# Fourier sums and folds in parts of 128 tokens behind each transposed block, and masked scores with their row minimum from one VectorE operation per head pair

## The chip, the cores and the metric

One core of one Trainium2 chip runs the whole program. The metric is the time of one execution on the device, in microseconds (us); the kernel before was timed in three runs.

## What is computed

Three layers follow each other: attention over a window of 64 tokens (4 batches, 8 heads, 576 tokens, 64 columns per head), a Fourier layer with a multilayer perceptron, and a gated perceptron. Cut to what matters here:

```python
scores = np.where((rel >= 0) & (rel < 64), 0.125 * (q @ k.T), -1e9)
attn = np.exp(scores - scores.max(-1, keepdims=True))
attn = attn / (attn.sum(-1, keepdims=True) + 1e-9)
x = (attn @ v), heads side by side                # [4, 576, 512]
u = x + real(fft(fft(x, axis=1), axis=2))         # tokens, then columns
un = (u - mean(u)) / sqrt(var(u) + 1e-6)
y = u + max(un @ w_ch1, 0) @ w_ch2
```

and a second perceptron with a gate over the tokens follows on `y`.

## The kernel before

The first stage, about a fifth of the time, runs attention as the main lane (`attention`, L303) and two other lanes that fill it: the decoding of the first weights, and the Fourier layer and normalization (`dft`, L439, and `ln`, L577) of the batches that are done. `drive` (L1060) interleaves the lanes by costs that the generators yield, and a list scheduler then sets the final order on each engine. Each engine's queue is worked in that order.

Attention goes through 36 blocks `n` of 64 queries, nine per batch. `scores(n)` (L308) lets TensorE (PE) compute four head pairs of 128 x 128 scores into one tile `sc`; VectorE (DVE) scales and masks all four at once (L317, 128 x 512) and takes the row maximum, negated, of all four at once (L320); ScalarE (ACT) then runs four exponentials with that maximum as bias (L322). `transposes` (L325) turns the four results on PE into `pt`, and ACT copies them (L331). `pv` (L334) multiplies two blocks with the values, `norm` (L346) divides on DVE, and `xt` (L365) transposes 128 finished tokens (64 for the last part of a batch, so five parts per batch) into the one PSUM tile `xt`, from which ACT copies them into `uT` (L373). `uT` holds all tokens with the 512 columns on four slices of 128 partitions.

`dft(b)` begins when all of batch b stands in `uT`. DVE makes the sums `E` and differences `O` of the two column halves over all 576 tokens (L448, L449: 128 x 1152), then folds the token axis in place (L452, L464: 128 x 576). ACT and GpSimd (POOL) split each result into two float32r parts, `eh`/`el` and `oh`/`ol` (L457, L458, L465, L466). One row more, `grow`, comes from `O` over POOL, ACT and POOL (L461 to L463). Then PE does the first Fourier stage: for each of three token groups a sum of seven matrix products (L482 with `grow` first, then six over `mm3`, L124 to L126) and then one of six with `oh`. The copies of these sums, `cp`, are written over `E` and `O` (L490). The second stage (L496) ends in `mi` and `pl`, which are added into `uT` (L512 to L521).

After the attention stage come the two perceptrons, which fill the rest with matrix products.

Of the kernel before, what the change touches and what calls it, by code (L numbers as in the profile page):

```python
# [13 lines left out]
ALU = mybir.AluOpType  # L14
# [93 lines left out]
class Kernel:  # L108
# [194 lines left out]
    def attention(self):  # L303
# [4 lines left out]
        def scores(n):  # L308
            b, j = divmod(n, NB)
            q, k = self.qt.pop((b, j)), self.kt[b, j // 3]  # L310
            sc = ps.tile([128, 4, 128], F32, tag="sc", bufs=2, name="sc")
            for hp in range(4):
                o = 64 * (j % 3)
                nc.tensor.matmul(sc[:, hp], lhsT=q[:, hp].rearrange("p a b -> p (a b)"), rhs=k[:, hp, o:o + 128], start=True, stop=True)  # L314
            mx = p.tile([128, 4], F32, tag="mx", bufs=3, name="mx")
            s = p.tile([128, 4, 128], F32, tag="s", bufs=SB, name="s")
            nc.vector.scalar_tensor_tensor(  # L317
                out=s, in0=sc, scalar=0.125, in1=self.mask[:, int(j == 0)].unsqueeze(1).to_broadcast([128, 4, 128]),
                op0=ALU.mult, op1=ALU.add)
            nc.vector.tensor_reduce(out=mx, in_=s, axis=AX.X, op=ALU.max, negate=True)  # L320
            for hp in range(4):
                nc.scalar.activation(out=s[:, hp], in_=s[:, hp], func=AF.Exp, bias=mx[:, hp:hp + 1])  # L322
            st[n], st['mx'] = s, mx
# [41 lines left out]
        def xt(n):  # L365
# [6 lines left out]
            t0 = S * b + 128 * i  # L372
            nc.scalar.activation(out=self.uT[:, :, t0:t0 + m], in_=t[:, :, 0:m], func=AF.Copy)  # L373
            if j == NB - 1:
                self.xdone = b
# [35 lines left out]
    def open_dft(self):  # L411
        nc = self.nc
        self.dp, self.dft_es = self.pool("dft", side="left")
        p = self.dp
        self.xdone = -1
        w = [516, 516, 512, 512, 258, 870, 870, 870, 870]
# [15 lines left out]
    def load_tables(self, i, after):  # L432
# [4 lines left out]
        self.tc.keep_in_program_order(self.nc.gpsimd.dma_start(self.tab[:, c], self.aps["tab"][:, c]))  # L437

    def dft(self, b):  # L439
        nc, p = self.nc, self.dp  # L440
        x = self.uT[:, :, S * b:S * b + S]
        V, G, A = nc.vector, nc.gpsimd, nc.scalar
        EF = G if b in FP else V
        row = p.tile([1, S], F32, tag="row", name="row")
        nc.sync.dma_start(row, x[0:1, 2])
        E = p.tile([128, 2, S], F32, tag="E", name="E")
        O = p.tile([128, 2, S], F32, tag="O", name="O")
        EF.tensor_tensor(out=E, in0=x[:, 0:2], in1=x[:, 2:4], op=ALU.add)  # L448
        EF.tensor_tensor(out=O, in0=x[:, 0:2], in1=x[:, 2:4], op=ALU.subtract)  # L449
        fold = lambda t: t[:, :, 1:289]  # L450
        rev = lambda t: t[:, :, 575:287:-1]
        EF.tensor_tensor(out=fold(E), in0=fold(E), in1=rev(E), op=ALU.add)  # L452
        eh = p.tile([128, 2, 290], F32R, tag="eh", name="eh")
        el = p.tile([128, 2, 290], F32R, tag="el", name="el")
        oh = p.tile([128, 2, 290], F32R, tag="oh", name="oh")
        ol = p.tile([128, 2, 290], F32R, tag="ol", name="ol")
        A.activation(out=eh[:, :, 0:289], in_=E[:, :, 0:289], func=AF.Copy)  # L457
        G.tensor_tensor(out=el[:, :, 0:289], in0=E[:, :, 0:289], in1=eh[:, :, 0:289], op=ALU.subtract)  # L458
        gr = p.tile([1, 290], F32, tag="gr", name="gr")
        G.tensor_copy(gr[:, 0:1], O[0:1, 0, 0:1])  # L460
        G.tensor_tensor(out=gr[:, 1:289], in0=O[0:1, 0, 1:289], in1=O[0:1, 0, 575:287:-1], op=ALU.add)  # L461
        A.activation(out=self.grow[0:1, 0:289], in_=gr[:, 0:289], func=AF.Copy)
        G.tensor_tensor(out=self.grow[32:33, 0:289], in0=gr[:, 0:289], in1=self.grow[0:1, 0:289], op=ALU.subtract)  # L463
        EF.tensor_tensor(out=fold(O), in0=fold(O), in1=rev(O), op=ALU.subtract)  # L464
        A.activation(out=oh[:, :, 0:289], in_=O[:, :, 0:289], func=AF.Copy)  # L465
        G.tensor_tensor(out=ol[:, :, 0:289], in0=O[:, :, 0:289], in1=oh[:, :, 0:289], op=ALU.subtract)  # L466
        yield 5000
# [6 lines left out]
        for which in range(2):  # L474
            for i, (t0, t1) in enumerate(ts):
# [3 lines left out]
                if which:  # L479
                    self.mm3(ps[:m, 0:n], [(oh[:, c, t0:t1], ol[:, c, t0:t1], self.sdh[:, c], self.sdl[:, c]) for c in range(2)])  # L480
                else:
                    nc.tensor.matmul(ps[:m, 0:n], lhsT=self.grow[:, t0:t1], rhs=self.gt, start=True, stop=False)  # L482
                    self.mm3(ps[:m, 0:n], [(eh[:, c, t0:t1], el[:, c, t0:t1], self.cdh[:, c], self.cdl[:, c]) for c in range(2)], first=False)
                if i < 2:
                    hi, lo = (bh, bl) if which else (ah, al)
                    hi, lo = hi[:, i, 0:n], lo[:, i, 0:n]
                else:
                    t = bt if which else at
                    hi, lo = t[0:33, 0:n], t[64:97, 0:n]
                cp = (O if which else E)[:m, i // 2, 288 * (i % 2):288 * (i % 2) + n]  # L490
                A.activation(out=cp, in_=ps[:m, 0:n], func=AF.Copy)
                A.activation(out=hi, in_=cp, func=AF.Copy)
                G.tensor_tensor(out=lo, in0=cp, in1=hi, op=ALU.subtract)
                yield 1700

        def stage2(out, lo_, hi_, tail, ch, cl, sl):  # L496
# [846 lines left out]
```

## Time and profile before

| | |
|---|---|
| median of 3 runs | 779.79 us (777.94 to 780.92) |
| the profiled execution | 780.66 us, of which 778.9 us are the span from the first to the last instruction |
| PE busy | 755.9 us, 97% of the span |
| DVE busy | 491.1 us, 63% |
| ACT busy | 340.5 us, 44% |
| POOL busy | 219.2 us, 28% |
| mean granted TensorE clock | 0.991 |

An engine's busy time is the time in which it had an instruction under way; matrix products overlap each other in the record, so a busy PE is not PE at its peak. [...] A wait names the instruction whose end released the waiting one.

### The profile page before, as it was taken

How to read it: one execution, taken by the hardware profiler on the slowest of the kernel's cores; microseconds unless marked ns; L12 is line 12 of the kernel's file. 1: busy time of each engine (PE TensorE's matmuls, PEld its weight loads, DVE VectorE, ACT ScalarE, POOL GpSimd, SP SyncE). 2: the span in 40 equal slices, each digit the busy share in tenths (PEclk: the TensorE clock that was granted, in tenths of full speed). 3: DMA queues.
4: the chain of work that ended last, by engine and by line, in shares of the span. 5: the costliest groups of instructions: out<-in, count | busy, mean ns of one | idle time of the engine just before them, and what ended most of it. 6: DMA issues, size and time to landing. Idle time of an engine off the chain costs nothing.

```text
span 778.9 us, 13646 instructions
## 1 busy us (share of the span) xinstructions
PE 755.9 (97%) x5018; PEld 727.3 (93%) x5018; DVE 491.1 (63%) x1126; ACT 340.5 (44%) x807; POOL 219.2 (28%) x268
## 2 busy tenths in 40 slices
PE   8879899999999999999999999999999999999998
PEld 7779688889999999999999999999999898989898
DVE  5677959594346489794588767644700468574662
ACT  5678797764233666341235323322742343130310
POOL 2135535534203551053712111121591021010100
PEclk9989999999999999999999999999999999999999
DMA  9996672353005878567746943953410020204023
GB/s 275 341 257 182 202 213 69 107 164 122 1 1 157 290 237 322 194 243 262 256 180 232 341 171 104 363 230 109 133 56 1 0 70 12 72 21 142 7 75 121
DMA packets 84770, 123.35 MB, mean 158 GB/s; under 512 B 24416, under 2 KB 61664, under 8 KB 84704
## 3 DMA queue, kind: packets, MB, share of 16 engines
q1 hardware_dynamic: 82912, 119.13, 46.0%
q0 software_dynamic: 576, 2.97, 1.2%
q8 instruction: 39, 0.64, 0.3%
q10 hardware_dynamic: 1216, 0.39, 0.2%
q14 instruction: 27, 0.22, 0.1%
HBM read 91.79 MB, written 30.67 MB: 157 GB/s over the span
## 4 chain that ended last, share of the span: by engine, by line
PE 82%; DVE 7%; DMA 6%; issue 2%; ACT 1%; POOL 0%; SPq 0%; DVEq 0%; ACTq 0%; POOLq 0%
PE w L124 7%; PE w L126 7%; PE w L125 7%; PE g L124 6%; PE c L124 6%; PE c L125 6%; PE c L126 6%; PE g L126 6%; PE g L125 6%; PE pv L342 3%; PE sc L314 3%; PE acc L126 2%; PE acc L125 2%; PE h L124 2%; PE acc L124 2%; PE h L126 2%
## 5 line engine op out<-in xcount | busy, mean ns | idle before, releaser
L164 ACT ACTIVATE set<-dec_w 128x256 fp32r<-128x256 f32 x103 | 41.7, 413 | 62.5 <-PE w L125 27.3
L798 POOL TENSOR_TENSOR u<-u 128x384 f32<-128x384 f32 x15 | 17.7, 1178 | 157.7 <-ACT u L797 139.0
L572 POOL TENSOR_TENSOR rq<-rq,mhalf 128x1 f32<-128x1 f32 (+1 forms) x24 | 15.7, 656 | 163.8 <-DVE rq L571 161.4
L322 ACT ACTIVATE s<-s,mx 128x128 f32<-128x128 f32 x144 | 46.2, 391 | 15.5 <-DVE mx L320 15.4
L158 ACT ACTIVATE dec_g<-dec_s 128x256 f32<-128x256 f32 x88 | 37.5, 429 | 32.9 <-DMA dec_s<-in_wi 16.7
L126 PE MATMUL acc<-rh,set 128*128 128x384 f32 x144 | 48.7, 338 | 0.0
L125 PE MATMUL acc<-rl,set 128*128 128x384 f32 x144 | 48.4, 336 | 0.0
L124 PE MATMUL acc<-rh,set 128*128 128x384 f32 x144 | 47.6, 337 | 0.5 <-DVE uT L655 0.5
L1004 DVE BATCH_NORM_STATS2 st<-u 128x6 f32<-128x512 f32 x18 | 12.4, 692 | 48.6 <-ACT u L1000 48.6
L160 DVE SCALAR_TENSOR_TENSOR dec_w<-dec_g,dec_w 128x256 int32<-128x256 int32 x88 | 41.3, 475 | 2.7 <-ACT dec_g L158 2.2
L314 PE MATMUL sc<-k,q 128*128 128x128 f32 x288 | 40.5, 290 | 2.5 <-DMA k<-in_k 1.4
L798 DVE TENSOR_TENSOR u<-w,u 128x384 f32<-128x384 f32 x44 | 24.3, 552 | 29.4 <-POOL u L798 24.3
L165 DVE TENSOR_TENSOR set<-dec_w,set 128x256 fp32r<-128x256 f32 x83 | 36.8, 451 | 8.2 <-PE h L125 3.8
L314 PEld LDWEIGHTS sc<-k,q 128*128 128x128 f32 x288 | 37.1, 203 | 4.0 <-DVE s L317 1.8
L317 DVE SCALAR_TENSOR_TENSOR s<-sc,mask 128x512 f32<-128x512 f32 x36 | 24.6, 686 | 25.4 <-PE pt L329 14.5
L159 DVE TENSOR_SCALAR dec_w<-dec_s 128x256 int32<-128x256 int32 x88 | 32.3, 377 | 6.4 <-DMA dec_s<-in_wi 3.9
L845 DVE TENSOR_TENSOR uT<-g,uT 128x384 f32<-128x384 f32 x36 | 19.3, 554 | 24.8 <-PE g L126 24.6
L670 DVE SCALAR_TENSOR_TENSOR rl<-h,rh 128x384 fp32r<-128x384 f32 x36 | 19.7, 548 | 20.1 <-ACT rh L669 20.1
L342 PEld LDWEIGHTS pv<-v,pts 128*64 128x64 f32 x576 | 24.7, 147 | 8.0 <-issue 4.5
L342 PE MATMUL pv<-v,pts 128*64 128x65 f32 x576 | 30.0, 237 | 1.6 <-DMA v<-in_v 1.6
L797 ACT ACTIVATE u<-w 128x384 f32<-128x384 f32 x29 | 14.1, 485 | 36.4 <-PE w L126 35.1
L655 DVE TENSOR_TENSOR uT<-acc,uT 128x384 f32<-128x384 f32 x48 | 25.2, 549 | 5.9 <-PE acc L126 5.7
(357 smaller groups left out, 2639.9 us busy)
## 6 DMA issues: line engine op xcount, KB each, us to landing
dec_s<-in_w SPq DMA_DIRECT2D x64, 256.0 KB, 3.3
v<-in_v SPq DMA_DIRECT2D x16, 520.0 KB, 5.4
xht<-xb SPq DMA_DIRECT2D x10, 768.0 KB, 10.0
xhm<-xb SPq DMA_DIRECT2D x10, 768.0 KB, 8.2
xlm<-xb SPq DMA_DIRECT2D x8, 768.0 KB, 9.2
k<-in_k SPq DMA_DIRECT2D x11, 512.0 KB, 5.7
xf<-u SPq DMA_DIRECT2D x18, 256.0 KB, 3.2
p<-xf SPq DMA_DIRECT2D x24, 192.0 KB, 3.6
```

The source lines that it names most:

```text
L124: mm(out, lhsT=lh, rhs=rh, start=first and i == 0, stop=False)
L125: mm(out, lhsT=lh, rhs=rl, start=False, stop=False)
L126: mm(out, lhsT=ll, rhs=rh, start=False, stop=last and i == n - 1)
L158: nc.scalar.activation(out=g, in_=s[:, :, 1].bitcast(F32), func=AF.Prelu, scale=2.0 ** -112, alpha=-2.0 ** 32)
L159: nc.vector.tensor_scalar(out=w, in0=s[:, :, 0], scalar1=29, scalar2=None, op0=ALU.logical_shift_right)
L160: nc.vector.scalar_tensor_tensor(out=w, in0=g[:].bitcast(I32), scalar=3, in1=w, op0=ALU.logical_shift_left, op1=ALU.bitwise_or)
L164: self.nc.scalar.activation(out=hi, in_=f, func=AF.Copy)
L165: (self.nc.gpsimd if self.bp is None else self.nc.vector).tensor_tensor(out=lo, in0=f, in1=hi, op=ALU.subtract)
L314: nc.tensor.matmul(sc[:, hp], lhsT=q[:, hp].rearrange("p a b -> p (a b)"), rhs=k[:, hp, o:o + 128], start=True, stop=True)
L322: nc.scalar.activation(out=s[:, hp], in_=s[:, hp], func=AF.Exp, bias=mx[:, hp:hp + 1])
L342: nc.tensor.matmul(o[r:r + 64, i // 4, 65 * (i % 4):65 * (i % 4) + 65], lhsT=pts[:, i // 2, 64 * (i % 2):64 * (i % 2) + 64], rhs=v[:, 65 * ...
L798: add = lambda eng, o, i, j: eng.tensor_tensor(out=o, in0=i, in1=j, op=ALU.add)
```

## The change

There are two parts.

**Scores.** In place of one masking and one maximum over four head pairs there are four operations, one per head pair, each of which adds the mask to the scores, multiplies by -0.125, writes the result and takes its row minimum. In the program each of these is two DVE instructions: one of 128 x 128, and one that writes the minimum, 128 x 1. The exponential has scale -1.

**Folds.** `folds` is called in `xt` for batches 0 to 2, behind the copy into `uT`. For each part of 128 (or 64) tokens `fold` makes `E` and `O` of those tokens, reading one column half from the PSUM tile `xt` and the other from `uT`, and folds the tokens whose partners are there: 96 in the third part, 128 in the fourth, 64 in the fifth. The folded `O` goes into a third tile, `F`. `fold_split` splits into float32r parts: behind the fourth part for tokens 65 to 288, if the first Fourier stage of the batch before has been written already, and behind the fifth for 0 to 64; else all at the start of `dft`. Batch 3 is folded at the start of `dft`, in whole. The product with `grow` becomes the last of its sum, and `cp` has a tile of its own with two buffers.

```diff
             s = p.tile([128, 4, 128], F32, tag="s", bufs=SB, name="s")
-            nc.vector.scalar_tensor_tensor(
-                out=s, in0=sc, scalar=0.125, in1=self.mask[:, int(j == 0)].unsqueeze(1).to_broadcast([128, 4, 128]),
-                op0=ALU.mult, op1=ALU.add)
-            nc.vector.tensor_reduce(out=mx, in_=s, axis=AX.X, op=ALU.max, negate=True)
+            mask = self.mask[:, int(j == 0)]
             for hp in range(4):
-                nc.scalar.activation(out=s[:, hp], in_=s[:, hp], func=AF.Exp, bias=mx[:, hp:hp + 1])
+                nc.vector.tensor_tensor_reduce(out=s[:, hp], in0=sc[:, hp], in1=mask, scale=-0.125, scalar=1e30, op0=ALU.add, op1=ALU.min, accum_out=mx[:, hp:hp + 1])
+            for hp in range(4):
+                nc.scalar.activation(out=s[:, hp], in_=s[:, hp], func=AF.Exp, bias=mx[:, hp:hp + 1], scale=-1.0)
...
             nc.scalar.activation(out=self.uT[:, :, t0:t0 + m], in_=t[:, :, 0:m], func=AF.Copy)
+            self.folds(b, i, t)
...
+    def fold(self, b, x, t, t0, m):
...
+        c = slice(t0, t0 + m)
+        V.tensor_tensor(out=E[:, :, c], in0=t, in1=x, op=ALU.add)
+        V.tensor_tensor(out=O[:, :, c], in0=t, in1=x, op=ALU.subtract)
+        a, z = max(1, S + 1 - t0 - m), min(289, S + 1 - t0)
+        if a < z:
+            r = slice(S - a, S - z, -1)
+            V.tensor_tensor(out=E[:, :, a:z], in0=E[:, :, a:z], in1=E[:, :, r], op=ALU.add)
+            V.tensor_tensor(out=F[:, :, a:z], in0=O[:, :, a:z], in1=O[:, :, r], op=ALU.subtract)
+            G.tensor_tensor(out=gr[:, a:z], in0=O[0:1, 0, a:z], in1=O[0:1, 0, r], op=ALU.add)
+        if t0 + m == S:
+            V.tensor_copy(F[:, :, 0:1], O[:, :, 0:1])
+            G.tensor_copy(gr[:, 0:1], O[0:1, 0, 0:1])
+
+    def fold_split(self, b, a, z):
...
+        A.activation(out=eh, in_=E[:, :, a:z], func=AF.Copy)
+        G.tensor_tensor(out=el, in0=E[:, :, a:z], in1=eh, op=ALU.subtract)
+        A.activation(out=oh, in_=F[:, :, a:z], func=AF.Copy)
+        G.tensor_tensor(out=ol, in0=F[:, :, a:z], in1=oh, op=ALU.subtract)
+        if a == 0:
...
+            A.activation(out=self.grow[0:1, 0:289], in_=gr, func=AF.Copy)
+            G.tensor_tensor(out=self.grow[32:33, 0:289], in0=gr, in1=self.grow[0:1, 0:289], op=ALU.subtract)
+
+    def folds(self, b, i, t):
+        if b == B - 1:
+            return
+        t0, m = 128 * i, 64 if i == 4 else 128
+        self.fold(b, self.uT[:, 2:4, S * b + t0:S * b + t0 + m], t[:, 0:2, 0:m], t0, m)
+        if i == 3 and self.dft_read == b - 1:
+            self.fold_split(b, 65, 289)
+        elif i == 4 and b in self.fp:
+            self.fold_split(b, 0, 65)
...
     def dft(self, b):
...
+        if b == B - 1:
+            self.fold(b, x[:, 2:4], x[:, 0:2], 0, S)
+        if b not in self.fp:
+            self.fold_split(b, 0, 289)
...
-                    nc.tensor.matmul(ps[:m, 0:n], lhsT=self.grow[:, t0:t1], rhs=self.gt, start=True, stop=False)
-                    self.mm3(ps[:m, 0:n], [(eh[:, c, t0:t1], el[:, c, t0:t1], self.cdh[:, c], self.cdl[:, c]) for c in range(2)], first=False)
+                    self.mm3(ps[:m, 0:n], [(eh[:, c, t0:t1], el[:, c, t0:t1], self.cdh[:, c], self.cdl[:, c]) for c in range(2)], last=False)
+                    nc.tensor.matmul(ps[:m, 0:n], lhsT=self.grow[:, t0:t1], rhs=self.gt, start=False, stop=True)
...
+                cp = p.tile([128, 258], F32, tag="cp", bufs=2, name="cp")[:m, 0:n]
```

How the order of the engines changes shows best at the first Fourier layer, that of batch 0. These are PE's rows there before: the transposes of the last 64 tokens of batch 0 (`xt`, 128x64), then attention, then the first two Fourier sums, each begun by its product with `grow` (L482).

```order
L371 MATMUL xt<-ident,x 128x64 x4
L329 MATMUL pt<-ident,s 128x128 x4
L342 MATMUL pv<-v,pts 64x65 x16
L314 MATMUL sc<-k,q_106 128x128 x8
L329 MATMUL pt<-ident,s 128x128 x4
L482 MATMUL g<-tab,grow 128x258
L124 MATMUL g<-tab,eh 128x258
L125 MATMUL g<-tab,eh 128x258
L482 MATMUL g<-tab,grow 128x258
```

And these are PE's rows at the same place now; L328, L341, L370 and L514 are the old L329, L342, L371 and L482.

```order
L370 MATMUL xt<-ident,x 128x64 x2
L314 MATMUL sc<-k,q_105 128x128 x8
L328 MATMUL pt<-ident,s 128x128 x4
L341 MATMUL pv<-v,pts 64x65 x16
L328 MATMUL pt<-ident,s 128x128 x4
L124 MATMUL g<-tab,eh 128x258
L125 MATMUL g<-tab,eh 128x258
...
L126 MATMUL g<-tab,el 128x258
L514 MATMUL g<-tab,grow 128x258 x2
```

The two sums begin with `eh` and end with `grow`, and they stand two attention blocks earlier (behind the scores of ring `q_105`, where `q_106` stood). On DVE the rows between the last part of batch 0 and its Fourier layer were these before:

```order
L159 TENSOR_SCALAR dec_w<-dec_s 128x256 x2
L448 TENSOR_TENSOR E<-uT 128x1152
L449 TENSOR_TENSOR O<-uT 128x1152
L320 TENSOR_REDUCE mx<-s 128x4
L160 SCALAR_TENSOR_TENSOR dec_w<-dec_g,dec_w 128x256 x2
L452 TENSOR_TENSOR E<-E 128x2x288
L357 TENSOR_SCALAR rc<-pv 128x8
L464 TENSOR_TENSOR O<-O 128x2x288
```

and are these now, where L319 is the new score operation, of which two instructions make one head pair:

```order
L450 TENSOR_TENSOR E<-xt,uT 128x2x64
L451 TENSOR_TENSOR O<-xt,uT 128x2x64
L455 TENSOR_TENSOR E<-E 128x2x64
L319 ISA s,mx<-sc,mask 128x128
L319 ISA mx 128x1
L456 TENSOR_TENSOR F<-O 128x2x64
```

The four long operations have become four short ones over the last 64 tokens; those of the first 512 tokens stand further ahead, between the attention blocks.

## Rows read from the trace of the kernel before

**Rows 1.** Busy time by stretch: us, then busy us (instructions) per engine, clock, DMA, GB/s
```profile
core 0: us, PE busy (x) PEld busy (x) DVE busy (x) ACT busy (x) POOL busy (x), PEclk, DMA share, GB/s
0.00:165.00 165.00, 147.16 (x1431) 131.02 (x1432) 120.33 (x241) 120.68 (x318) 69.18 (x110) 0.96 0.69 203
165.00:780.00 615.00, 608.72 (x3589) 596.25 (x3588) 370.77 (x886) 219.80 (x490) 149.97 (x159) 1.00 0.42 146
```

**Rows 2.** PE's timeline: start us, us, instructions, [us idle before, and the releaser]
```profile
50.46 0.58 PE L482 MATMUL g<-tab,grow 128*128 128x258 f32 x1 [4.24 <-POOL grow L463]
...
90.62 1.20 PE L329 MATMUL pt<-ident,s 128*128 128x128 f32 x4 [1.20 <-ACT s L322]
92.92 1.63 PE L314 MATMUL sc<-k,q 128*128 128x128 f32 x8 [1.10 <-DVE s L317]
```

**Rows 3.** Chain of waits, 32 to 58 us: start us, us, what
```profile
35.45 1.82 PE sc L314 x16
37.27 0.44 PE pt L329 x4
37.71 1.07 PE pv L342 x16
...
46.60 1.28 ACT s L322 x4
...
49.62 0.80 POOL grow L463
...
51.04 0.21 PE g L124
...
56.65 0.12 PE g L124
```

**Rows 4.** Busy time by stretch around PE's longest wait
```profile
45.00:50.00 5.00, 1.22 (x12) 0.98 (x10) 5.00 (x10) 3.40 (x10) 2.60 (x4) 0.91 1.08 288
50.00:55.00 5.00, 4.54 (x20) 4.24 (x20) 2.37 (x5) 2.92 (x9) 3.85 (x5) 0.50 0.75 229
```

**Rows 5.** Busy time by stretch: attention, and two parts of it
```profile
10.00:135.00 125.00, 111.86 (x1155) 98.94 (x1155) 94.82 (x188) 97.23 (x267) 51.04 (x76) 0.95 0.75 222
...
80.00:98.00 18.00, 14.55 (x140) 11.83 (x139) 17.22 (x37) 13.17 (x36) 10.41 (x12) 0.91 0.62 178
123.00:134.00 11.00, 9.48 (x96) 7.99 (x94) 10.82 (x24) 9.21 (x26) 7.36 (x10) 1.00 0.21 69
```

**Rows 6.** DVE's groups by form: xcount | busy us, mean ns | idle before, releasers
```profile
L317 DVE SCALAR_TENSOR_TENSOR s<-sc,mask 128x512 f32<-128x512 f32 x36 | 24.6, 686 | 25.4 <-PE pt L329 14.5 <-PE sc L314 8.6 <-ACT bh L492 1.7
L320 DVE TENSOR_REDUCE mx<-s 128x4 f32<-128x512 f32 x36 | 24.4, 681 | 1.0
...
L574 DVE TENSOR_TENSOR rq<-rq,rq 128x1 f32<-128x1 f32 x18 | 2.8, 153 | 0.5
...
L1039 DVE TENSOR_TENSOR xl<-p,xh 128x64 fp32r<-128x64 f32 x4 | 0.9, 217 | 0.0
```

**Rows 7.** ACT's groups by form, columns as in Rows 6, 0 to 165 us
```profile
L331 ACT ACTIVATE pts<-pt 128x512 f32<-128x512 f32 x36 | 21.1, 587 | 7.4 <-PE pt L329 7.2
...
L373 ACT ACTIVATE uT<-xt 128x256 f32<-128x256 f32 x4 | 1.5, 380 | 0.5 <-PE xt L371 0.3
```

**Rows 8.** DVE's timeline: two score blocks, then the last folds of batch 0
```profile
7.79 0.69 DVE L317 SCALAR_TENSOR_TENSOR s<-sc,mask 128x512 f32<-128x512 f32 x1 [5.30 <-PE sc L314]
8.51 0.69 DVE L320 TENSOR_REDUCE mx<-s 128x4 f32<-128x512 f32 x1
9.12 1.41 DVE L317 SCALAR_TENSOR_TENSOR s<-sc,mask 128x512 f32<-128x512 f32 x2
...
48.13 0.15 DVE L357 TENSOR_SCALAR rc<-pv 128x8 f32<-128x8 f32 x1
48.21 0.74 DVE L464 TENSOR_TENSOR O<-O 128x576 f32<-128x576 f32 x1
48.87 0.68 DVE L317 SCALAR_TENSOR_TENSOR s<-sc,mask 128x512 f32<-128x512 f32 x1
```

More of the change, by code (lines that the diff above doesn't have):

```diff
@@ L414, in open_dft @@
         p = self.dp
-        self.xdone = -1
+        self.xdone, self.dft_read = -1, -1
+        self.eo, self.fp, self.gr = {}, {}, {}
         w = [516, 516, 512, 512, 258, 870, 870, 870, 870]
@@ L437, in load_tables @@
         self.tc.keep_in_program_order(self.nc.gpsimd.dma_start(self.tab[:, c], self.aps["tab"][:, c]))
+    def fold(self, b, x, t, t0, m):
+        V, G = self.nc.vector, self.nc.gpsimd
+        if t0 == 0:
+            self.eo[b] = [self.dp.tile([128, 2, S], F32, tag=n, name=n) for n in ("E", "O", "F")]
+            self.gr[b] = self.dp.tile([1, 290], F32, tag="gr", name="gr")
+        E, O, F = self.eo[b]
+        gr = self.gr[b]
+        c = slice(t0, t0 + m)
[11 more added lines that the diff above has]
+    def fold_split(self, b, a, z):
+        G, A = self.nc.gpsimd, self.nc.scalar
+        E, _, F = self.eo[b]
+        if b not in self.fp:
+            self.fp[b] = [self.dp.tile([128, 2, 290], F32R, tag=n, name=n) for n in ("eh", "el", "oh", "ol")]
+        eh, el, oh, ol = (q[:, :, a:z] for q in self.fp[b])
+        A.activation(out=eh, in_=E[:, :, a:z], func=AF.Copy)
[3 more added lines that the diff above has]
+        if a == 0:
+            gr = self.gr[b][:, 0:289]
+            A.activation(out=self.grow[0:1, 0:289], in_=gr, func=AF.Copy)
[9 more added lines that the diff above has]
+            self.fold_split(b, 0, 65)
     def dft(self, b):
@@ L442, in dft @@
         V, G, A = nc.vector, nc.gpsimd, nc.scalar
-        EF = G if b in FP else V
         row = p.tile([1, S], F32, tag="row", name="row")
         nc.sync.dma_start(row, x[0:1, 2])
[L446 to L466, printed above, removed]
+        if b == B - 1:
+            self.fold(b, x[:, 2:4], x[:, 0:2], 0, S)
+        if b not in self.fp:
+            self.fold_split(b, 0, 289)
+        eh, el, oh, ol = self.fp[b]
         yield 5000
@@ L489, in dft @@
                     hi, lo = t[0:33, 0:n], t[64:97, 0:n]
-                cp = (O if which else E)[:m, i // 2, 288 * (i % 2):288 * (i % 2) + n]
+                cp = p.tile([128, 258], F32, tag="cp", bufs=2, name="cp")[:m, 0:n]
                 A.activation(out=cp, in_=ps[:m, 0:n], func=AF.Copy)
@@ L494, in dft @@
                 yield 1700
+        self.dft_read = b
         def stage2(out, lo_, hi_, tail, ch, cl, sl):
```

## The prediction, made before the changed kernel was run

> **What bounds the kernel now.** I read the busy times by stretch first [rows 1]. Behind 165 us PE is busy for 608.7 of 615 us and its clock is full: the change moves nothing out of there that could matter, since PE's products stay the same in number and DVE has room. Ahead of 165 us PE is busy for 147.16 us, so it idles for 17.8, and its clock is 0.96. DVE is busy for 120.33 of the 165, ACT for 120.68. Whatever the change gains or loses comes from this first stretch, and the most it could gain is the 17.8 us idle and some 6 us of clock, less the start.
>
> PE's timeline says where it idles [rows 2]. The longest wait, 4.24 us, is that of the first Fourier product of batch 0 for `grow`. The chain of waits [rows 3] comes to it over ACT and over POOL's `grow` at 49.62, and over DVE's `E` and `O` before that: in 45 to 50 us DVE is busy throughout and PE for 1.22 us [rows 4]. Behind that wait the clock stands at 0.50, the lower level, in 50 to 55 us, and the same Fourier product takes 0.21 us there and 0.12 at 56.65 [rows 3, 4]. The next waits are a cluster in 80 to 98 us, where DVE is busy 17.22 of 18 us, PE 14.55, and the clock is 0.91; and one in 123 to 134, where DVE is busy 10.82 of 11 and PE 9.48 [rows 5]. Both hold the four long folds of the next batch, among DVE's other work. So in these three places DVE, or a chain that begins on it, is the bound; between them PE is.
>
> **The changed parts and their costs.** The profiled execution took 780.66 us, 0.87 above the median of 779.79; the sum is made against it, and 0.87 is taken off at the end.
>
> *The wait for `grow` (A).* In the new order PE has, behind the last `xt` of batch 0, eight score products (two records each), two `pt` groups and a `pv` group before the first Fourier product: 1.82 + 2 x 0.44 + 1.07 = 3.8 us of cover [rows 3]. What must happen meanwhile: the copy to `uT` (0.38 [rows 7]) and two sums and a fold of 64 tokens on DVE (0.2 to 0.3 each, by the line worked out under B); on ACT six exponentials and a `pts` copy stand ahead of `eh` (6 x 1.28/4 [rows 3] and 0.59 [rows 7]), then `eh` itself, about the size of an exponential (0.3). The slower of the two ways is ACT's, 0.38 + 1.92 + 0.59 + 0.3 = 3.2 us, and nearer 4 where an exponential waits for its minimum. The first Fourier product is hardly late. Behind it come `el` and `grow` on POOL, 0.80 for `grow` [rows 3] and about as much for `el`, against twelve products of 0.12 us = 1.44 that stand ahead of `grow` now. With hand-offs I leave 1.5 us of idle time: 2.7 gained. The clock then should fall less often. It costs 0.5 x 4.54 = 2.3 us in 50 to 55 [rows 4]; I count half, 1.1. A = 3.8.
>
> *The cluster at 80 to 98 us (B).* Idle 18 - 14.55 = 3.45, clock 0.09 x 14.55 = 1.3 [rows 5]: 4.8 us. Here the four long operations of batch 1 leave DVE, which now come earlier in parts. A fold of 576 elements takes 0.66 us from start to start (48.21 to 48.87), and with 1.05 ns per element, from 217 ns at 64 elements and 686 at 512 [rows 6], the 1152 of `E` or `O` take 1.27: 3.9 us leave, 0.8 stay for the last 64 tokens. 3.1 of 17.2 us is much, but the parts go into 55 to 80 us, among attention that needs DVE too. I count half: B = 2.4.
>
> *The stretch at 123 to 134 us (C).* Idle 1.5, full clock [rows 5]. Batch 2's parts move ahead in the same way: C = 1.0.
>
> *The folds themselves.* By the same line a part of 256 elements takes 0.32 us from start to start, 192 take 0.26, 128 take 0.19. Per batch: twice 4 x 0.32 + 0.19, twice 0.26 + 0.32 + 0.19, and a copy at 0.08, in all 4.6 us against 3.9: 0.7 x 3 = 2.1 us more DVE. `xt` is held until DVE has read it; the next transposes into it come two blocks later, so I cost that at nothing; if DVE were over 2 us behind, PE's `xt` rows would wait.
>
> *The scores (D).* A masking and a maximum take 8.51 - 7.79 = 0.72 and 9.12 - 8.51 = 0.61, so 1.33 us per block from start to start [rows 8]. Now there are four pairs of instructions. The 128-wide one is bounded by 217 + 64 x 1.05 = 284 ns [rows 6] if it must end first, and 0.19 from start to start if the next overlaps its end. No row shows the one that writes a minimum. Its bounds are the 153 ns of a 128 x 1 operation [rows 6] and the 0.08 us after which `rc`, 150 ns long, lets the fold behind it start [rows 8]. A pair costs 0.27 to 0.44 us, a block 1.08 to 1.75: from -9.0 to +15.1 us of DVE over 36 blocks. The minimum needs the last element, so I take 0.284 for the first; it reads no tile and no wait stands in front of it, so it is nearest to `rc`: 0.08. A pair is 0.365, a block 1.46, the sum +4.7.
>
> [...]
>
> DVE's 4.7 + 2.1 = 6.8 us more lie beside PE's work where DVE has room; where it has none, they count. The two full stretches are 29 of the 125 us of attention [rows 5]: 0.23 x 6.8 = 1.6 lost. Exponentials can begin after one pair, 0.37 us, and not after 1.33; ACT's own work is the same, and where PE waits for them this is in B already.
>
> Sum: 3.8 + 2.4 + 1.0 - 1.6 = 5.6 us. 780.66 - 5.6 = 775.1, less 0.87: **774.2 us**. A measurement of this kernel can tell 0.5%, 3.9 us, from no change, so faster means below 775.9.
>
> **The rivals.**
> 1. *DVE becomes the bound (slower).* A pair costs 0.44 us: 15.1 + 2.1 = 17.2 us more on 94.82 of 125 [rows 5], 112, that is 90% of the stretch on a queue worked in order. A stays; B and C are lost, because the full stretches stay full; 0.23 x 17.2 = 4.0 is added in them, and I count half of the other 13.2, 6.6, since half of DVE's free time elsewhere stands behind waits for PE (14.5 us for `pt` and 8.6 for `sc` [rows 6]). 780.66 - 3.8 + 4.0 + 6.6 = 787.5, so 786.6. It decides from about 0.40 us per pair, between 5.6 gained at 0.365 and 6.8 lost at 0.44. For it: no row has the operation. Against it: `rc`. [...]
> 2. *The loads take A's place (no change).* In 45 to 50 us the DMA engines have a share of 1.08 at 288 GB/s [rows 4]; blocks that come 4 us sooner would wait for keys and values. A falls away: 780.66 - 1.8 = 778.9, so 778.0. For it: the share. Against it: from 50 us on the share is 0.75 and falls, and the Fourier products need no load.
> 3. *All three places close (faster still).* A pair costs 0.27: DVE gets 9.0 - 2.1 = 6.9 us free. A is 4.2 + 2.3 - 0.5 = 6.0, B 4.8, C 1.5: 12.3, so 780.66 - 12.3 - 0.87 = 767.5. For it: DVE's short operations do overlap. Against it: more and shorter instructions on three queues.
> 4. *The change does not do what it says for batch 2:* the order has its split in one piece. That is only a part of C and stands in the forecast.
>
> **How the numbers follow.** Forecast 0.40, by itself 771 to 778; rival 1 0.23, rival 2 0.20, rival 3 0.17. The range goes from 765, between rivals 3 and the forecast's end with room for rival 3, to 787, the price of rival 1. Faster: most of the forecast, 0.34, rival 3, and a little of rival 2: 0.53. Within 0.5%: the rest of the forecast, most of rival 2 and the edge of rival 1: 0.27. Slower: 0.20 of rival 1.
>
> **What would show it.** Right: the first Fourier product behind batch 0 waits under 2 us; the clock's 0.50 is gone or shorter; PE's idle time ahead of 165 us is near 11 us; DVE in the same stretch is busy for some 7 us more; a score pair's two instructions start 0.28 and 0.08 us before their successors. Wrong by rival 1: pairs of 0.40 us and more, DVE near 9 tenths from 40 to 140 us and PE's waits for `s` or for exponentials longer than the 1.20 and 1.10 of now [rows 2]. By rival 2: PE waits for `v` or `k` around 45 to 60 us. By rival 3: no wait of PE over 0.5 us from 40 to 135 us. The forecast falls, too, if PE behind 165 us loses more than 2 us to a new order there.

## The result and the profile after

| | before | changed |
|---|---|---|
| median of six runs each, us | 780.12 (777.94 to 781.01) | 770.24 (769.20 to 772.94) |
| profiled execution, us (span) | 780.66 (778.9) | 772.72 (770.9) |
| ratio to before, 95% interval | | 0.9882 [0.9859, 0.9905] |

The change makes the kernel 9.9 us faster. The page of the changed kernel:

```profile
span 770.9 us, 13909 instructions
...
PE 750.4 (97%) x5018; PEld 723.3 (94%) x5018; DVE 486.0 (63%) x1382; ACT 340.6 (44%) x811; POOL 219.7 (28%) x278
...
PEclk9999999999999999999999999999999999999999
...
PE 90%; DVE 5%; ACT 3%; DMA 1%; issue 1%; SPq 0%; POOL 0%; ACTq 0%; DVEq 0%; POOLq 0%
```

PE's share of the chain is 90%. Its busy time by stretch in the changed kernel, with the columns of rows 1:

```profile
0.00:165.00 165.00, 149.34 (x1476) 134.98 (x1477) 120.94 (x522) 125.85 (x337) 70.76 (x120) 0.99 0.72 214
165.00:770.00 605.00, 601.02 (x3544) 588.37 (x3542) 365.03 (x861) 214.76 (x475) 148.90 (x158) 1.00 0.42 146
35.00:40.00 5.00, 4.97 (x36) 4.83 (x36) 3.09 (x15) 1.05 (x2) 2.86 (x4) 0.66 0.98 353
45.00:50.00 5.00, 4.69 (x65) 4.09 (x61) 2.85 (x13) 5.00 (x17) 3.08 (x6) 1.00 1.04 273
50.00:55.00 5.00, 5.00 (x52) 4.87 (x47) 3.53 (x21) 4.36 (x14) 3.20 (x7) 1.00 0.93 335
10.00:135.00 125.00, 114.46 (x1249) 101.98 (x1250) 89.64 (x438) 99.93 (x274) 53.04 (x89) 0.99 0.77 226
80.00:98.00 18.00, 14.15 (x167) 11.99 (x163) 15.15 (x77) 17.08 (x47) 7.82 (x15) 1.00 0.80 222
123.00:134.00 11.00, 11.00 (x125) 9.05 (x125) 6.86 (x24) 6.67 (x16) 2.03 (x4) 1.00 0.15 50
```

Against [rows 1, 4, 5]: in 45 to 50 us PE is busy for 4.69 us where it was 1.22, and in 50 to 55 the clock is 1.00 where it was 0.50. The stretch from 123 us is full. That from 80 us is not: PE idles there for 3.85 us (3.45 before), at full clock now. ACT in place of DVE is the fullest engine, but the rows of PE's four waits there, below, name DVE three times, for 3.36 us, and ACT once, for 0.49. Behind 165 us nothing moved that matters. PE's timeline in the changed kernel, with the columns of rows 2:

```profile
35.03 1.12 PE L341 MATMUL pv<-v,pts 128*64 128x65 f32 x16 [2.37 <-ACT s L321]
...
45.96 0.37 PE L124 MATMUL g<-tab,eh 128*128 128x258 f32 x1
...
47.49 0.41 PE L514 MATMUL g<-tab,grow 128*128 128x258 f32 x2
...
83.66 0.66 PE L328 MATMUL pt<-ident,s 128*128 128x128 f32 x4 [0.49 <-ACT pts L330]
...
85.23 0.41 PE L370 MATMUL xt<-ident,x 128*128 128x128 f32 x2 [0.92 <-DVE x L360]
...
90.80 1.16 PE L314 MATMUL sc<-k,q 128*128 128x128 f32 x8 [1.67 <-DVE mx L319]
...
97.59 1.16 PE L314 MATMUL sc<-k,q 128*128 128x128 f32 x8 [0.77 <-DVE mx L319]
```

The wait of 4.24 us [rows 2] is gone: neither the first Fourier product (45.96) nor the products with `grow` (47.49) wait. In its place the longest wait is 2.37 us at 35 us, with the half clock behind it (0.66 in 35 to 40 us, 0.50 in 37 to 39). Its row names an exponential that ended just then, but these products read only `pts` and `v`. The timelines of ACT and of SyncE, which issues the loads, have both:

```profile
29.40 0.60 ACT L330 ACTIVATE pts<-pt 128x512 f32<-128x512 f32 x1 [0.23 <-ACT uT L372]
```

```profile
22.93 1.20 SPq L282 DMA_DIRECT2D v<-in_v  x1
```

`pts` was there at 30.00 us. The load of `v`, issued at 22.93 us, landed 12.0 us later (view of the tile `v`), at 34.9: PE waited for a load. In PE's timeline before, its longest wait for a load was this one:

```profile
32.40 2.00 PE L342 MATMUL pv<-v,pts 128*64 128x65 f32 x32 [1.62 <-DMA v<-in_v]
```

And the beginning of DVE's timeline, the first score block of the changed kernel:

```profile
6.62 0.29 DVE L319 CUSTOM_DVE_ANT_0 s<-sc,mask 128x128 f32<-128x128 f32 x1 [4.14 <-PE sc L314]
6.84 0.08 DVE L319 DVE_READ_ACCUMULATOR2_ANT mx<- 128x1 f32 x1
6.84 0.28 DVE L319 CUSTOM_DVE_ANT_0 s<-sc,mask 128x128 f32<-128x128 f32 x1
7.05 0.08 DVE L319 DVE_READ_ACCUMULATOR2_ANT mx<- 128x1 f32 x1
```

A score pair takes 0.21 to 0.22 us from start to start: the 128-wide instruction, 0.29 long, lets the next begin before its end, and the one that writes the minimum begins together with the next pair's first. A block takes 0.84 us, not the 1.33 of before [rows 8].

**Where the time went.** I added up two losses of PE over windows of 1 us of each profiled execution: the idle time, and the busy time times one less the granted clock. Each cell is idle + clock, in us; S, P and G are the parts of the change as the next section names them.

```
                     0-30    30-60   60-80   80-100 100-130 130-165 | sum
before             4.1+0.0 6.0+4.2 0.0+0.0 3.7+1.7 0.3+0.0 3.8+0.0 | 23.8
changed (S P G)    5.7+0.0 3.1+1.7 0.3+0.0 3.8+0.0 0.4+0.0 2.3+0.0 | 17.3
S                  4.3+0.0 3.4+1.4 0.0+0.0 3.9+2.5 0.7+0.0 1.8+0.0 | 18.0
P                  5.8+0.0 4.0+1.5 0.9+0.0 2.8+1.6 1.2+0.0 4.3+1.7 | 23.8
G                  4.8+1.7 4.2+0.0 0.3+0.0 3.1+1.6 0.6+0.0 3.3+0.0 | 19.6
P G                5.4+0.0 4.4+0.0 0.6+0.0 2.1+0.0 1.1+0.0 2.1+0.0 | 15.7
S G                4.5+0.0 3.2+0.0 0.0+0.0 4.0+1.7 0.2+0.0 3.2+0.0 | 16.8
S P                5.1+1.6 2.4+0.0 1.2+0.0 1.8+0.0 0.2+0.0 4.6+3.1 | 20.0
```

From before to the changed kernel 6.5 of the 8.0 us by which the spans differ show here: 5.4 at the first Fourier layer (30 to 60 us), 1.6 at 80 to 100, 1.5 behind 130, less 1.6 lost ahead of 30 us, of which 1.1 are longer waits for the loads of `q` and `k` (1.38 us before, 2.50 now). Of the other 1.5, 0.3 is idle time behind 165 us (5.2 us before, 4.9 now), and the rest no view places (span less losses lies between 752.9 and 755.8 us in these eight). The median gained more than the profiled executions, because the clock varies from run to run: span times one less the run's mean clock is 0.6 us on average in the changed kernel's six runs, and 5.4 in one series of 23 runs of before.

### The profile page after: what moved, and what is told of

Its sections match the earlier page's. It is cut to its first block, busy times and chain, and to the rows that moved or that the text cites. A ratio compares the mean times of both kernels' runs of the same rounds, so it can differ in the third digit from the quotient of the medians.

```text
span 770.9 us, 13909 instructions
## 1 busy us (share of the span) xinstructions
PE 750.4 (97%) x5018; PEld 723.3 (94%) x5018; DVE 486.0 (63%) x1382; ACT 340.6 (44%) x811; POOL 219.7 (28%) x278
## 4 chain that ended last, share of the span: by engine, by line
PE 90%; DVE 5%; ACT 3%; DMA 1%; issue 1%; SPq 0%; POOL 0%; ACTq 0%; DVEq 0%; POOLq 0%
PE w L124 7%; PE w L126 7%; PE w L125 7%; PE g L124 7%; PE g L126 6%; PE g L125 6%; PE c L124 6%; PE c L125 6%; PE c L126 6%; PE acc L126 3%; PE acc L125 3%; PE h L124 3%; PE h L125 3%; PE acc L124 3%; PE h L126 3%; PE sc L314 3%
## 5 line engine op out<-in xcount | busy, mean ns | idle before, releaser
L605 POOL TENSOR_TENSOR rq<-rq,mhalf 128x1 f32<-128x1 f32 (+1 forms) x24 | 15.7, 654 | 157.8 <-DVE rq L604 155.6
L319 DVE CUSTOM_DVE_ANT_0 s<-sc,mask 128x128 f32<-128x128 f32 x144 | 33.4, 285 | 22.0 <-PE sc L314 13.8
L165 DVE TENSOR_TENSOR set<-dec_w,set 128x256 fp32r<-128x256 f32 x83 | 37.8, 462 | 10.8 <-ACT set L164 4.3
L160 DVE SCALAR_TENSOR_TENSOR dec_w<-dec_g,dec_w 128x256 int32<-128x256 int32 x88 | 42.1, 481 | 3.5 <-ACT dec_g L158 2.8
L159 DVE TENSOR_SCALAR dec_w<-dec_s 128x256 int32<-128x256 int32 x88 | 32.3, 373 | 6.1 <-DMA dec_s<-in_wi 3.2
L703 DVE SCALAR_TENSOR_TENSOR rl<-h,rh 128x384 fp32r<-128x384 f32 x36 | 19.8, 551 | 23.1 <-ACT rh L702 23.1
L341 PEld LDWEIGHTS pv<-v,pts 128*64 128x64 f32 x576 | 23.5, 137 | 9.3 <-issue 4.2
L341 PE MATMUL pv<-v,pts 128*64 128x65 f32 x576 | 29.1, 226 | 2.8 <-ACT s L321 2.4
```

The costliest lines, as they stand in the source:

```text
L160: nc.vector.scalar_tensor_tensor(out=w, in0=g[:].bitcast(I32), scalar=3, in1=w, op0=ALU.logical_shift_left, op1=ALU.bitwise_or)
L165: (self.nc.gpsimd if self.bp is None else self.nc.vector).tensor_tensor(out=lo, in0=f, in1=hi, op=ALU.subtract)
L319: nc.vector.tensor_tensor_reduce(out=s[:, hp], in0=sc[:, hp], in1=mask, scale=-0.125, scalar=1e30, op0=ALU.add, op1=ALU.min, accum_out=mx[ ...
L341: nc.tensor.matmul(o[r:r + 64, i // 4, 65 * (i % 4):65 * (i % 4) + 65], lhsT=pts[:, i // 2, 64 * (i % 2):64 * (i % 2) + 64], rhs=v[:, 65 * ...
```

## The experiments

Theory F: the gain comes from the folds, which end the wait for `grow` and the half clock behind it. Theory S: it comes from the cheap score operation. Three edits can be told apart: **S**, the score operation; **P**, sums and folds in token parts, with the tiles that go with them (`F`, and `cp` on its own), which weren't tried apart; **G**, the product with `grow` at the end of its sum (before, at its start). Each kernel was timed on the same chip as runs of the kernel before, and its ratio is to those; medians of different experiments come from different chips, so a difference of theirs is given by the ratios, too. The rows are of each kernel's timeline, of the engine named in them, unless another view is named.

**S alone** (`s_only`): the kernel before, with the first hunk of the diff.

> The kernel before with the new score operation alone; folds, grow and cp as before. Theory F (the gain of 9.9 us comes from the folds in parts: PE's 4.24 us wait for grow and the half clock behind it go): this kernel keeps that wait, so 778 to 781 us, and the half clock stays in three places. Theory S (it comes from the score operation, whose pair starts 0.21 us after the one before, so that DVE loses 36 x (1.33 - 0.84) = 17.6 us, and whose first minimum is there after 0.3 us): 771 to 774 us, with the wait for grow still near 4 us. If the two need each other: 775 to 778 us.

771.53 us, 0.9896 [0.9866, 0.9926]. That is theory S's time. One part brings nearly the whole gain, although PE still waits for `grow` in its timeline:

```profile
44.68 0.58 PE L481 MATMUL g<-tab,grow 128*128 128x258 f32 x1 [2.91 <-POOL grow L462]
```

**P and G** (`f_only`): the changed kernel with the old masking and maximum.

> The change with the old masking and maximum over four head pairs; folds in parts, grow last and cp of its own stay. Theory F: 771 to 774 us, no wait for grow over 1.5 us, clock 0.50 at one place at most. Theory S: 778 to 781 us, since DVE then has 2 us more than in the kernel before. If the two need each other: 775 to 778 us.

772.04 us, 0.9908 [0.9878, 0.9938]; no wait for `grow`. That is theory F's time. The other part alone brings nearly the whole gain, too. Together they would have made 18 us; they make 9.9. Neither F nor S can be right alone.

**G alone** (`g_last`), in the kernel before:

```diff
-matmul(ps, lhsT=self.grow[:, t0:t1], rhs=self.gt, start=True, stop=False)
-self.mm3(ps, [(eh, el, ...)], first=False)
+self.mm3(ps, [(eh, el, ...)], last=False)
+matmul(ps, lhsT=self.grow[:, t0:t1], rhs=self.gt, start=False, stop=True)
```

> The kernel before with one edit: the product with grow stands last in its sum. Theory F in its narrow form (what counts is that the first Fourier sum need not wait for grow, the last thing ready): the 4.24 us wait falls to 3 us or less and the time to 776 to 778 us. If the folds themselves were late as well (eh came at 49.40 us, grow at 50.41, by the profile of before), only about 1 us goes: 779 us.

777.72 us, 0.9963 [0.9946, 0.9980]. In PE's timeline the wait is 2.87 us and on `eh`:

```profile
48.36 0.39 PE L124 MATMUL g<-tab,eh 128*128 128x258 f32 x1 [2.87 <-ACT eh L457]
```

**S and P** (`g_first`): the changed kernel with the hunk above undone.

> The change with one part undone: the product with grow stands first in its sum again. Theory F in its narrow form: the wait for grow is back with 1 to 2 us and a stretch of half clock, 773 to 775 us. If the parts have made grow early enough: 769 to 771 us, as the change itself.

777.03 us, 0.9954 [0.9936, 0.9972]. That is 6.8 us more than the changed kernel (5.6 by the ratios), which neither theory had. PE's timeline has a wait for `grow` of under 1 us; much of the loss is at another place, 100 us later:

```profile
44.75 0.40 PE L513 MATMUL g<-tab,grow 128*128 128x258 f32 x1 [0.98 <-POOL grow L475]
...
145.63 0.69 PE L124 MATMUL h<-xh,set 128*128 128x384 f32 x1 [4.02 <-DVE rl L703]
```

There PE changes over from attention to the perceptron. Its next product needs `rl`, and DVE does batch 3's whole sums and folds first, among weight decodes. In the changed kernel `rl` stands behind the same sums and folds, yet other products stand in PE's order there, and PE waits for 1.46 us. Behind the 4.02 us the clock is 0.50 (the last number but two, of the view by stretch):

```profile
146.00:150.00 4.00, 4.00 (x14) 4.00 (x14) 2.78 (x11) 4.00 (x9) 0.00 (x0) 0.50 0.41 131
```

**A pair as dear as rival 1 had it** (`fill4`): the changed kernel with a write that nobody reads.

```diff
                 nc.vector.tensor_tensor_reduce(out=s[:, hp], in0=sc[:, hp], in1=mask, ...)
+                nc.vector.memset(self.fill, 0.0)
```

> The changed kernel with a write of 128 x 230 zeros into a tile that nobody reads behind each score pair. It should take 0.24 us, by 1.05 ns per element, so that a pair takes 0.21 + 0.24 = 0.45 us from start to start, which is what the prediction's rival 1 gave the pair; a block takes 1.8 us in place of 0.84, and DVE gets 144 x 0.24 = 35 us more in the attention. Theory DVE (the kernel is near DVE's bound there, and the pair's low price is what the gain rests on): 783 to 790 us, PE waiting for minima by 1 us and more at many places. Theory other bound (after the change, loads, ACT and hand-offs set what is left of PE's idle time, and DVE has room): 771 to 776 us, that is under 6 us lost.

778.08 us, 0.9968 [0.9949, 0.9988]. The row of these writes among DVE's groups, columns as in rows 6:

```profile
L321 DVE MEMSET fill<- 128x230 f32 x144 | 36.0, 250 | 6.8
```

36 us more on DVE cost 7.8 us (6.7 by the ratios), between the two theories, and the kernel is still faster than before. So DVE's time has a price, but at 0.46 us per pair (0.21 + 0.25) the kernel doesn't become slower than before. The order sets some of these writes in a row ahead of a block, so this is a near likeness of a dear pair, not the thing itself.

**All minima first** (`allmin`): the exponentials read a copy of the four minima.

```diff
+            my = p.tile([128, 4], F32, tag="my", bufs=3, name="my")
+            nc.vector.tensor_copy(my, mx)
...
-                nc.scalar.activation(..., bias=mx[:, hp:hp + 1], scale=-1.0)
+                nc.scalar.activation(..., bias=my[:, hp:hp + 1], scale=-1.0)
```

> The changed kernel with a copy of the four minima (128 x 4) behind the four pairs, which the exponentials read in place of the minima themselves: each of them then waits for all four pairs and the copy, about 1.0 us, not 0.21. It costs DVE about 0.1 to 0.15 us per block, 5 us at most. Theory latency (the gain of the score part comes from exponentials that begin after one pair): the time returns to that of the folds alone, 772 us or more. Theory DVE time (it comes from the 17.6 us that DVE no longer spends on masks and minima): 770 to 772 us. The two lie near each other; the waits of PE for ACT's exponentials and of ACT for DVE tell more than the time.

783.09 us, 1.0024 [1.0011, 1.0037], 11 us above the 772 at which theory latency begins. The copy takes 0.284 us in the mean, 10.2 in all, and 8.9 us of loss lie at the change-over, where PE waits 4.65 us for `rl`. What the late exponentials cost by themselves isn't settled by it: in `f_only` they also wait for a whole block's minima, 1.33 us, at 772.04.

**Batch 3 in parts, too** (`b3`): the two places that leave it out are gone.

```diff
     def folds(self, b, i, t):
-        if b == B - 1:
-            return
...
-        if b == B - 1:
-            self.fold(b, x[:, 2:4], x[:, 0:2], 0, S)
```

> The changed kernel with batch 3, too, summed and folded in token parts; only its split stays at the start of its Fourier layer. At the switch from attention to the perceptron all kernels so far have PE waiting for DVE's rl (1.46 us in the changed kernel, 4.02 with half clock behind it in the one with the product with grow first), and what stands ahead of it on DVE there is batch 3's long sums of 1.36 and 1.35 us. Theory place (each kernel's time is set by a few such waits, which the order makes or unmakes): that wait shrinks below 1 us and the time is 767 to 770 us. Theory spread (the wait is taken over by the next late thing, the split on POOL or the weights): 769.5 to 772 us.

773.33 us, 0.9901 [0.9882, 0.9921]: no gain, and above the times of both theories. In PE's timeline the one wait became three, with 5.3 + 1.7 us lost in 130 to 165 us in place of 2.3:

```profile
137.54 0.43 PE L370 MATMUL xt<-ident,x 64*128 64x64 f32 x4 [1.57 <-DVE rq L603]
145.38 0.79 PE L124 MATMUL acc<-rh,set 128*128 128x384 f32 x3 [1.85 <-ACT rh L698]
153.09 0.45 PE L124 MATMUL h<-xh,set 128*128 128x384 f32 x1 [1.78 <-DVE rl L699]
```

**Less for ACT** (`pool_hi`): in the attention, one copy per decoded weight on POOL.

```diff
-        self.nc.scalar.activation(out=hi, in_=f, func=AF.Copy)
+        if self.bp is None:
+            self.nc.gpsimd.tensor_copy(hi, f)
+        else:
+            self.nc.scalar.activation(out=hi, in_=f, func=AF.Copy)
```

> The changed kernel with one copy of each weight that is decoded during the attention taken from ACT to POOL. ACT is busy for 100 of the 125 us of the attention, and 5.00 of 5 us at 45, 80 and 95 us; POOL is busy for 53. Theory ACT (in place of DVE, ACT is now the bound where PE idles at 80 to 98 us): 766 to 769 us, with PE's idle time there well below 3.85 us. Theory no single bound: 769 to 773 us, since the waits pass to DVE or to POOL, whose copies are slower.

773.27 us, 0.9901 [0.9883, 0.9919]. The losses ahead of 130 us fall from 15.0 us to 9.9, and PE is busy for 16.52 of 18 us at 80 to 98, ACT for 15.89 (14.15 and 17.08 without this edit). Over the whole kernel ACT is busy for 7.6 us less (333.0 for 340.6) and POOL for 8.2 more (227.9 for 219.7). So work taken from ACT shortens waits there, though in the changed kernel 3.36 of the 3.85 us idle name DVE. And S with P loses little at 80 to 100 us without this edit, so an order alone can do it too: that ACT is the bound there is not shown. The change-over takes 5.7 us in place of 2.3, with a wait of 3.05 us for `rl`, and the total is no better. By stretch:

```profile
80.00:98.00 18.00, 16.52 (x199) 14.20 (x200) 14.57 (x81) 15.89 (x43) 7.36 (x16) 1.00 0.86 229
```

**One small copy off DVE** (`fcopy`, on the changed kernel, and `pool_fc`, on `pool_hi`). In the changed kernel DVE's timeline ahead of `rl`, and then POOL's:

```profile
144.27 0.75 DVE L456 TENSOR_TENSOR F<-O 128x576 f32<-128x576 f32 x1
144.94 1.29 DVE L459 COPY F<-O 128x2 f32<-128x2 f32 x1
...
146.81 0.55 DVE L703 SCALAR_TENSOR_TENSOR rl<-h,rh 128x384 fp32r<-128x384 f32 x1
```

```profile
144.28 1.92 POOL L469 TENSOR_TENSOR el<-E,eh 128x578 fp32r<-128x578 f32 x1
```

```diff
-            V.tensor_copy(F[:, :, 0:1], O[:, :, 0:1])
+            self.nc.scalar.activation(out=F[:, :, 0:1], in_=O[:, :, 0:1], func=AF.Copy)
```

> The changed kernel with one small copy (128 x 2, the first column of F) on ACT and not on DVE. For batch 3 it took 1.29 us on DVE, until POOL's el behind it ended, while elsewhere it took 0.17 to 0.20; it stands ahead of rl, for which PE waits 1.46 us at the switch to the perceptron. Theory switch (that place is set by what stands ahead of rl on DVE): PE's wait there falls below 0.6 us and the time to 768.5 to 769.8 us. Theory other: ACT's copy comes late itself, or rl waits for the next thing, the decodes, and the time is 770 to 771.5 us.

774.72 us, 0.9936 [0.9915, 0.9957], 4.5 us worse than the changed kernel (4.2 by the ratios). The copy is gone from DVE and `rl` comes later all the same: two decodes of weights take 2.12 us on DVE, beside two of POOL's operations, and PE waits 4.62 us (timelines of `fcopy`).

```profile
143.10 2.12 DVE L159 TENSOR_SCALAR dec_w<-dec_s 128x256 int32<-128x256 int32 x2
```

```profile
150.92 0.69 PE L124 MATMUL h<-xh,set 128*128 128x384 f32 x1 [4.62 <-DVE rl L703]
```

> The kernel with one copy per decoded weight on POOL, and that small copy on ACT. Taking the decode's copy from ACT brought PE's losses ahead of 130 us (idle time and half clock together) from 15.0 to 9.9 us, and the switch to the perceptron, 130 to 165 us, gave 3.4 back (2.3 to 5.7), with a wait for rl of 3.05 us and half clock behind it. Theory switch: with the 1.28 us of the small copy gone that wait falls to 1.8 us, the clock stays full, and the time is 768 to 771 us, 2 to 5 below the kernel with the decode's copy alone. Theory order (what stands ahead of rl is settled anew by each order): 772 to 774 us again.

772.85 us, 0.9906 [0.9881, 0.9930], against 773.27 without: the wait is 1.86 us, as worked out, but the clock falls behind it (0.50 in 143 to 145 us), and the times don't differ beyond their spread. So what the change-over costs isn't set by one operation; each order settles it anew.

**S and G** (`s_glast`): the kernel before with those two edits.

> The kernel before with the new score operation and with the product with grow at the end of its sum; the folds stay long and whole at the start of each Fourier layer. With the score operation alone the first Fourier product still waited 2.91 us for grow. Theory keys (the place behind batch 0 is one loss that any of the three edits takes most of, so they do not add up): 769 to 773 us, like the score operation alone (771.5), with that wait now on eh and between 1 and 3 us. Theory parts (only folds in token parts take the wait and the half clock together): at most 1 us better than 771.5, and the mean clock of its runs stays near 0.996, where the change has 1.000. If it is below 769 us, the folds in parts cost more than they bring.

772.21 us, 0.9893 [0.9874, 0.9912]. With folds still long and whole, PE's waits at the first Fourier layer are smaller than either theory said; the time is that of theory keys:

```profile
42.54 0.39 PE L124 MATMUL g<-tab,eh 128*128 128x258 f32 x1 [0.26 <-ACT eh L456]
...
43.94 0.39 PE L126 MATMUL g<-tab,el 128*128 128x258 f32 x1 [0.65 <-POOL el L457]
```

**P alone** (`p_only`): `f_only` with the product with `grow` first.

> The changed kernel with the old masking and maximum and with the product with grow at the start of its sum: of the three edits only the folds in parts are left. It completes the table of the three (score operation S, parts P, product last G): none 780.9, S 771.5, G 777.7, PG 772.0, SP 777.0, SG 772.2, all three 770.2. Theory keys (each edit alone takes most of the loss at the first Fourier product): that wait is under 3 us, as it was with each of the other edits alone, and the time without the clock's share is 769.5 to 773.5 us, against 775.0 of before; the time itself 771 to 777, by what the switch to the perceptron takes. Theory pairs (parts need the product last, which alone lets eh cover grow): the wait stays above 3 us and the time is 777 us or more.

777.68 us, 0.9962 [0.9950, 0.9975]. In PE's timeline the first wait is short, as theory keys had it, but the time is in the range of theory pairs. In the table of losses the change-over takes back 2.2 us of the gain, the start 1.7:

```profile
48.06 0.51 PE L514 MATMUL g<-tab,grow 128*128 128x258 f32 x2 [1.11 <-POOL grow L476]
...
148.86 0.44 PE L124 MATMUL h<-xh,set 128*128 128x384 f32 x1 [4.20 <-DVE rl L704]
```

The eight combinations, with the clock's share (span times one less the mean clock of the run; its mean over the runs) and the median of the times without it:

| edits | median us | ratio, 95% interval | clock's share | time without it |
|---|---|---|---|---|
| none | 780.97 | 1 | 5.4 | 775.2 |
| P | 777.68 | 0.9962 [0.9950, 0.9975] | 4.5 | 773.3 |
| G | 777.72 | 0.9963 [0.9946, 0.9980] | 3.9 | 773.6 |
| S, P | 777.03 | 0.9954 [0.9936, 0.9972] | 3.4 | 773.2 |
| S, G | 772.21 | 0.9893 [0.9874, 0.9912] | 1.3 | 770.7 |
| P, G | 772.04 | 0.9908 [0.9878, 0.9938] | 2.4 | 770.3 |
| S | 771.53 | 0.9896 [0.9866, 0.9926] | 3.1 | 768.8 |
| S, P, G | 770.24 | 0.9882 [0.9859, 0.9905] | 0.6 | 770.2 |

The rows come from several chips, and "none" is one series of before: in the runs of before beside P its clock's share was 6.1 us and the time without it 774.1, beside S with G 6.4 and 774.1. The ratios tell more than the last two columns. Four combinations lie within 2 us, and their intervals overlap. The changed kernel has the lowest median and the least clock loss, but these runs don't show that it beats S alone. No version run here has a lower median.

## Why the prediction was right, and where it was not

The time, 770.24 us, lies in the range and on the forecast's side, 4 us below the forecast. That it does is in part luck. The prediction gave the whole gain to the folds and a loss to the scores; the runs show 8.9 us for the folds with G, 9.4 for the scores alone, and 9.9 for both. Of the signs that it named, the first Fourier product waits under 2 us and the 0.50 of 50 to 55 us is gone; but PE's idle time ahead of 165 us is 15.7 us and not 11, and DVE is busy for 0.6 us more there and not 7. By its steps:

- **A was right in kind and short in the clock.** The wait for `grow` went, and further than worked out: of its 4.24 us nothing is left at the Fourier products, where 1.5 were allowed. That the idle time of 30 to 60 us fell by 2.9 us, near the 2.7 worked out, is luck: the wait for `v` there grew from 1.62 to 2.37 us, and two for `pts`, of 0.42 and 0.31, came new. No term stood for them. The clock gave 2.5 against 1.1, where "I count half" was the step that failed; what is left, 1.7, stands behind the wait for `v`. Over the runs it gave more still: the clock's share fell from 5.4 us, in the series above, to 0.6. The runs add what the prediction did not see: S, P or G alone brings this stretch from 10.2 us of loss to between 4.2 and 5.5. It is one loss that three edits reach. How each does it (a shorter queue on DVE, folds already done, cover for `grow`) is argued from the edits and not shown. That is one reason why the parts don't add up, and not the whole: P alone loses 4.2 us more than S at the change-over, and G's profiled run, its fastest at 774.23 us, doesn't place what its other runs lose.
- **B was wrong in its idle time.** "I count half" of 4.8 us; the idle time did not shrink in 80 to 98 us (3.85 us), and only the clock came back. DVE got room there, 15.15 of 18 us from 17.22, and ACT became the fullest at 17.08, yet PE's waits still name DVE for 3.36 us. From 82.9 to 91.9 us DVE is busy for 8.86 of 9.00 us, with weight decodes and the normalization's small operations among the scores: DVE had room in the whole of the stretch, and none where PE waited longest. With less work for ACT, in `pool_hi`, PE's idle time there fell to 1.5 us; which of the two bounds the place is open.
- **C was right in its number**, 1.5 us of idle time gone against 1.0, and not in its reason. Of batch 2's four long operations only the last fold (125.31 us in DVE's timeline before) lay in 123 to 134 us; the others stood at 117 to 122, where PE didn't wait. Its longest wait in the stretch, 1.05 us just ahead of 134, stood behind DVE's additions to `uT`. DVE is busy there for 6.86 of 11 us now, from 10.82; how much of that the parts did isn't shown.
- **D had the wrong sign.** The pair took 0.21 us, below the lower bound of 0.27: 36 x (1.33 - 0.84) = 17.6 us less for DVE, not 4.7 more. Two steps failed. The first is "The minimum needs the last element, so I take 0.284 for the first": the next pair began 0.21 us behind it, before its end, near the 0.19 of the overlapped bound. The second is the price of 0.08 us, from `rc`, for the instruction that writes the minimum: it begins together with the next pair's first and cost nothing. So of the 1.6 us taken off, 1.1 (0.23 x 4.7) went for nothing. DVE's busy time ahead of 165 us didn't fall all the same, since other work moved there: the weight decodes (L159, L160, L165) took 19.8 us of it before and take 29.2 now.
- **The folds themselves** were priced well. A part of 256 elements was to take 0.32 us from start to start, and in DVE's timeline the first two begin 0.34 us apart; their length of 0.42 is the 0.419 of the prediction's line. Only some folds that lay beside POOL's operations took far longer (the last section has one of 1.80 us), and no term stood for that.

```profile
20.45 0.42 DVE L450 TENSOR_TENSOR E<-xt,uT 128x256 f32<-128x256 f32 x1
20.79 0.41 DVE L451 TENSOR_TENSOR O<-xt,uT 128x256 f32<-128x256 f32 x1
```

- **Rival 1** fell with D. Its price was too high as well: with 36 us added on DVE the kernel took 778.08 us, not 786.6. It gave a pair 0.44 us, and the trace has 0.21: the second pair began at 6.84 us, before the first's 6.62 + 0.29 = 6.91.
- **Rival 2** didn't come where it was looked for, and came in part elsewhere. At 45 to 60 us PE waits for no load in the changed kernel, with a DMA share of 1.04 and 0.93. But ahead of that its waits for loads grew from 3.0 us (1.38 for `k`, 1.62 for `v`) to 4.9 (0.71 for `q`, 1.79 for `k`, 2.37 for `v`). That took 1.9 us of the gain, and not all of A.
- **Rival 3** had its condition (a pair of 0.27 or less) and not its time, 767.5, because B stayed open, the start lost 1.6 us and the wait for `v` remained. "No wait over 0.5 us" was not met.
- **Missing altogether** was the change-over at 135 to 160 us. Across the kernels run here its loss, idle and clock together, went from 1.8 us to 9.4 (`fcopy`), more than most edits were worth. It lay in the prediction's stretch, but as the change leaves batch 3 whole, no term stood for it.

Left open: why S alone escapes at the change-over while S with P does not, other than by the order; why the load of `v` took 12.0 us to land; and what waiting for all minima costs by itself.

## What to carry to other kernels

When several edits relieve one place, don't add their gains: work out which of them is enough, and what the place costs once it is relieved. Where a scheduler sets the order, an edit also reshuffles places it doesn't touch, so read each experiment by stretch and not by its total alone. Where a wait's row names something that the waiting instruction doesn't read, look up when its real inputs came, the loads above all. And price a short vector operation from start to start in a run of them, not by its length in the profile (here 0.21 us against 0.29).

## What the runs showed of the hardware

- An instruction that writes a row minimum, 82 ns in the mean, cost nothing from start to start: the next 128-wide instruction began at the same time (6.84 and 6.84 us).
- DVE's copy of 128 x 2 took 1.29 us beside POOL's `el` and ended with it (144.94 + 1.29 = 146.23; 144.28 + 1.92 = 146.20), while the same copy took 0.17 and 0.20 us for batches 0 and 1. In `fcopy` two decodes took 2.12 us and ended at 145.22 us, just behind POOL's second operation at 145.07, while in the changed kernel two took 1.11 and 1.09 us.
- A fold of batch 2 took 1.80 us on DVE, until 104.90 us, just behind POOL's operation that ended at 104.68 (rows of DVE and of POOL). In batch 0 a fold of the same size took 0.55 us.

```profile
103.10 1.80 DVE L456 TENSOR_TENSOR F<-O 128x192 f32<-128x192 f32 x1
```

```profile
103.39 1.29 POOL L648 TENSOR_TENSOR xl<-u,xh 128x512 fp32r<-128x512 f32 x1
```

- The half clock came and went between runs of one kernel: the mean clock lay between 0.988 and 0.998 in one series of 23 runs of before. In `g_first` 4.02 us of waiting at 141 us was followed by 0.50 in 146 to 150 us, and in `s_only` 2.91 us by 0.50 in 45 to 47, while in `g_last` 2.87 us was followed by full clock (1.00 from 48 to 60 us).
